# Gated linear attention and a maxout feed-forward on one core: the planner's load times, and when a small token group is opened

## The chip, the cores and the metric

The kernel runs on one core of a Trainium2 chip, in one launch. The metric is the device time of that launch in microseconds (us). The time before is 162.61 us, the median of three runs (162.48 to 163.09).

## The reference, cut to what matters

```python
# q, k, v, alpha: (4, 8, 768, 48) float32; w1, w2: (384, 1024); w_out: (1024, 384)
for t in range(S):
    state = alpha[:, :, t, :, None] * state + einsum('bhd,bhe->bhde', k[:, :, t], v[:, :, t])
    y[:, :, t] = einsum('bhd,bhde->bhe', q[:, :, t], state)
x = y.transpose(0, 2, 1, 3).reshape(3072, 384)
out = maximum(x @ w1, x @ w2) @ w_out
```

The first half is a recurrence over time with one state of 48 x 48 for each batch and head. The second half is a feed-forward over 3072 tokens.

## The kernel before, in words

**Chunks.** The recurrence is cut into 24 chunks of 128 time steps (six for each of four batches), all eight heads together. A chunk needs four loads of 192 KB (alpha, k, q, v: tiles `af`, `kf`, `qf`, `vf`), each with six buffers, issued from SP's queue at L184. The steps of chunk n, with the names that this text uses:

- a1(n), ACT, L252: the logarithm of alpha, `loga`. It is the first reader of the loads.
- p1(n), PE, L257 and L261: running sums of `loga`, `cs`. Then ACT makes two exponentials of it, `en` and `ep` (L267), and a small one, `gg` (L271).
- `kt` (POOL, L279) and `qt` (DVE, L276) scale k and q; POOL also casts v (L283).
- p2(n), PE, L316 and L318: transposes into `tp`; ACT or DVE copies them to `qk` (L393).
- p3(n), PE, L334: scores `pa`, `pb`; DVE masks them into `pt` (L353).
- kv(n), PE, L345: the chunk's addition to the state; DVE adds it (`w`, L364), POOL decays the state for the next chunk (L295, L303).
- p4(n), PE, L376 and L382: the output `y`; a3(n), ACT, L389, copies it into `xT`, the input of the feed-forward.

**Token groups.** The feed-forward uses max(a, b) = (a - b, floored at 0) + b: the weights w1 - w2 are made once (`wd`), and `m` = w2 @ w_out once. It runs over groups of one to three chunks. A group has eight steps f (PE, L429: three matmuls each into `h`, as wide as the group; then a relu on ACT, L436, or DVE, L434, into `g`), and for each chunk two steps t (PE): the first half has six matmuls (L443 and three of L446), the second five (L446), into `op`. `op` is evicted to `outs` (L393) and stored from SP's queue (L456). In this text f(i) and t(i) are numbered over the whole kernel, from 0 to 95 and from 0 to 23.

**What sets the order.** A small planner runs in Python when the kernel is built. It keeps a clock for each engine, gives every step a cost and a latency, and picks for each engine the step that can start first by its own sums; the earliest over all engines is emitted. Each engine then executes its instructions in that order, and waits where an input is not there. For SP the planner models a load as `LOAD` on a shared wire plus a latency `lat`. PE prefers steps of the recurrence; steps f and t have a high `prio` number and fill in. The function `refill` opens a token group when fewer than three steps of the last one are pending: it takes up to three chunks whose a3 is done, and as few as one.

Of the kernel before, what the change touches and what calls it, by code (L numbers as in the profile page):

```python
# [49 lines left out]
class Sched:  # L50
# [49 lines left out]
    def run(self):  # L100
        while True:
            c = self.pick("PE")
            if c and self.refill:
                self.refill(c[1])
            best = None
            for e in self.todo:
                c = self.pick(e)
                if c and (best is None or c[1] < best[0]):
                    best = (c[1], e, c[2])
            if best is None:  # L110
                if self.refill and self.refill(1e9):
                    continue
                break
            t, e, op = best
            cost = op.engs[e]
            if e == "PE" and op.tiled != self.tiled:
                cost += 0.09
                self.tiled = op.tiled
            if e == "SP":
                t = max(t, self.wire - 4.0)  # L120
                self.wire = max(self.wire, t + 0.7) + cost
                op.done = self.wire + op.lat
                cost = 0.45
            else:
                op.done = t + cost + op.lat
            self.free[e] = t + cost
            for b in op.alloc:
                b.ring.taken.append(b)
            for x in op.engs:
                self.todo[x].remove(op)  # L130
            op.fn(e)
        assert not any(self.todo.values()), {e: [(o.name, o.n) for o in v][:5] for e, v in self.todo.items()}
# [3 lines left out]
def kernel(  # L136
# [20 lines left out]
    C = 128  # L157
# [6 lines left out]
    WMAX = 384  # L164
# [15 lines left out]
    def load(n, i):  # L180
        b, c = divmod(n, NCH)
        src, tag = SRC[i]
        t = loads[n][i] = ldp.tile([128, H, D], FP32, tag=tag, name=tag)
        nc.sync.dma_start(out=t, in_=src[b, :, c * C : (c + 1) * C, :].rearrange("h p d -> p h d"))  # L184
# [58 lines left out]
    st = {n: {} for n in range(NCG)}  # L243
# [156 lines left out]
    def prep_t(f):  # L400
        tp = psx.tile([128, 2 * NP, 128], FP16, tag="x", name="wtp")
        for i in range(2):
            for s in range(3):
                nc.tensor.transpose(tp[:, 3 * i + s, :], w216[:, s, (f + i) * 128 : (f + i + 1) * 128], ident16)
        st["w2", f] = tp
# [18 lines left out]
    def fstep(a, W, f):  # L424
        if f == 0:
            gts[a] = mo.tile([128, NF, WMAX], FP16, tag="g16", name="g16", bufs=NG)
        h = hs[a, f] = psm.tile([128, WMAX], FP32, tag="m", name="h")
        for s in range(3):
            nc.tensor.matmul(h[:, 0:W], lhsT=wd16[:, s, f * 128 : (f + 1) * 128], rhs=xT[:, s, a : a + W],  # L429
                             start=(s == 0), stop=(s == 2))  # L430

    def relu(e, a, W, f):
        if e == "DVE":
            nc.vector.tensor_relu(gts[a][:, f, 0:W], hs[a, f][:, 0:W])  # L434
        else:
            nc.scalar.activation(out=gts[a][:, f, 0:W], in_=hs[a, f][:, 0:W], func=ACTF.Relu)  # L436

    def tstep(a, i, half):
        t0 = a + i * C
        if half == 0:  # L440
            op = ops[t0] = psm.tile([128, DM], FP32, tag="m", name="op")
            for s in range(3):
                nc.tensor.matmul(op, lhsT=xT[:, s, t0 : t0 + C], rhs=m16[:, s, :], start=(s == 0), stop=False)  # L443
        op = ops[t0]
        for f in (range(3) if half == 0 else range(3, NF)):
            nc.tensor.matmul(op, lhsT=gts[a][:, f, i * C : (i + 1) * C], rhs=wo16[:, f, :],  # L446
                             start=False, stop=(f == NF - 1))
# [3 lines left out]
    def oevict(e, t0):  # L451
        outs[t0] = mo.tile([128, DM], FP32, tag="outs", name="outs", bufs=NO)
        copy(e, outs[t0], ops[t0])

    def store(t0):
        nc.sync.dma_start(out=out[t0 : t0 + C, :], in_=outs[t0])  # L456
# [11 lines left out]
    def op(*a, **k):  # L468
        return Op(S, *a, **k)

    G = {n: {} for n in range(NCG)}

    def dep(n, name):
        return G[n].get(name) if n in G else None

    LOAD, WLOAD = 0.98, 3.9
    bl = {}

    def loads_of(n):
        bl[n] = [Buf(r) for r in rl]  # L480
        for i in range(4):
            G[n]["ld", i] = op("ld", n, {"SP": LOAD}, lambda e, n=n, i=i: load(n, i), lat=1.6, alloc=[bl[n][i]],
                               after=[G[n].get(("ld", i - 1)), dep(n - 1, ("ld", 3))], prio=n)

    loads_of(0)
    lw2 = op("w2", 0, {"SP": WLOAD}, lambda e: load_w2(), lat=1.6, after=[G[0]["ld", 3]], prio=0.5)
    prev = lw2
# [7 lines left out]
    for n in range(1, NCG):  # L495
        loads_of(n)
        if n == 1:
            G[1]["ld", 0].after.append(prev)
# [4 lines left out]
        for s, c in enumerate(({"ACT": 0.95}, {"DVE": 0.65}, {"POOL": 1.5}))  # L503
    ]
    wdc = [[op("wd", s, {"POOL": 1.2} if s == 2 else {"DVE": 0.68}, lambda e, s=s, i=i: prep_wd(e, s, i),
               deps=[lw1[i], lw2]) for s in range(3)] for i in range(2)]
# [4 lines left out]
    for f in range(0, NF, 2):  # L511
        b = Buf(rx)
        t = op("w2t", f, {"PE": 0.4}, lambda e, f=f: prep_t(f), lat=0.17, deps=w2c, alloc=[b], prio=500 + f)
# [3 lines left out]
    for s in range(3):  # L517
        b = Buf(rm)
        for i in range(2):
            prev = op("m", s, {"PE": 0.66}, lambda e, s=s, i=i: prep_m(s, i), lat=0.17,  # L520
                      deps=w2t + woc[2 * i : 2 * i + 2], after=[prev], alloc=[b] if i == 0 else (), prio=800 + s)
        mdone.append(op("mev", s, {"ACT": 0.4, "DVE": 0.45}, lambda e, s=s: copy(e, m16[:, s, :], mps[s]),
                        deps=[prev], reads=[b]))
# [4 lines left out]
    for n in range(NCG):  # L528
        c = n % NCH
# [28 lines left out]
        if c:  # L558
            pg = G[n - 1]
            add("g", {"POOL": 0.25}, lambda e, n=n: vg(n), [pg["gg"], g["gg"]], alloc=["g"], reads=[B_[n - 1]["gg"], "gg"])  # L560
            if c < NCH - 1:
                add("t32", {"POOL": 0.56}, lambda e, n=n: vt32(n), [g["g"], pg["w"]], alloc=["t32"],
                    reads=["g", B_[n - 1]["w"]])
            for t in range(2):
                add(f"T{t}", {"POOL": 0.56}, lambda e, n=n, t=t: vT(n, t), [g["g"], pg["w"]],
                    alloc=["T"] if t == 0 else (), reads=["g", B_[n - 1]["w"]] + (["T"] if t else []))
                if t:
                    g["T1"].after.append(g["T0"])
        if c < NCH - 1:
            add("kv", {"PE": 0.18}, lambda e, n=n: p3k(n), [g["kt"], g["v1"]], lat=0.17, alloc=["kv"], reads=["kt", "v"])  # L570
            add("w", {"DVE": 0.75}, lambda e, n=n: vw(n), [g["kv"], g.get("t32")], alloc=["w"],
                reads=["kv"] + (["t32"] if c else []))
        add("p4", {"PE": 0.54 if c else 0.37}, lambda e, n=n: p4(n), [g["m1"], g["v1"], g.get("T1")], lat=0.17,
            alloc=["y"], reads=["pt", "v", "qk"] + (["T"] if c else []), tiled=True)
# [3 lines left out]
    nxt = [0]  # L578
    pend = []

    def refill(now):
        while pend and pend[0].done is not None:
            pend.pop(0)
        if len([o for o in pend if o.done is None]) > 2 or nxt[0] >= NCG:
            return
        a = nxt[0]
        k = 0
        while k < WMAX // C and a + k < NCG and G[a + k]["a3"].done is not None and G[a + k]["a3"].done <= now + 0.3:
            k += 1
        if k == 0:  # L590
            return
        nxt[0] += k
        W, a0 = k * C, a * C
        bg = Buf(rg16)
        rel = []
        xs = [G[a + i]["a3"] for i in range(k)]
        for f in range(NF):
            bh = Buf(rm)
            o = op("f", a, {"PE": 3 * max(W / 2400 + 0.0025, 0.07)}, lambda e, a0=a0, W=W, f=f: fstep(a0, W, f),
                   lat=0.17, deps=xs + wdc[f // NFH], after=pend[-1:], alloc=[bh] + ([bg] if f == 0 else []), prio=1000 + a)  # L600
            pend.append(o)
            rel.append(op("relu", a, {"ACT": 0.08 + W / 1200, "DVE": 0.1 + W / 960},
                          lambda e, a0=a0, W=W, f=f: relu(e, a0, W, f), deps=[o], reads=[bh, bg], prio=n))
        for i in range(k):
            bo, bs = Buf(rm), Buf(ro)
            for half in range(2):
                o = op("t", a + i, {"PE": (0.98, 0.82)[half]}, lambda e, a0=a0, i=i, half=half: tstep(a0, i, half),
                       lat=0.17, deps=mdone + woc + (rel[:3] if half == 0 else rel), after=pend[-1:],
                       alloc=[bo] if half == 0 else (), reads=[bg] if half else [bg], prio=1000 + a)
                pend.append(o)  # L610
            ev = op("oev", a + i, {"ACT": 0.4, "DVE": 0.45}, lambda e, t=a0 + i * C: oevict(e, t), deps=[o],
                    alloc=[bs], reads=[bo], prio=n)
            op("st", a + i, {"SP": 0.5}, lambda e, t=a0 + i * C: store(t), lat=1.2, deps=[ev], reads=[bs], prio=-1)
        return True

    S.refill = refill
# [31 lines left out]
```

## Time and profile before

| | |
|---|---|
| median of the runs | 162.61 us |
| the profiled execution | 162.2 us |
| its span, first to last instruction | 160.3 us |
| PE busy | 138.6 us (86%) |
| ACT busy | 101.8 us (64%) |
| POOL busy | 87.6 us (55%) |
| DVE busy | 81.9 us (51%) |
| DMA queue of the loads and stores | 84.9% of 16 engines' span |
| mean granted TensorE clock | 0.968 |

Busy time counts instructions that run; an engine that stands in front of a semaphore is idle. The span is that of one execution; the 1.9 us around it belong to every run. PEld are the weight loads of TensorE, which run beside its matmuls. In rows of a timeline the first number is the start in us from the beginning of the span, the second how long it lasted; in brackets stands how long the engine was idle just before, and what ended that.

### The profile page before, as it was taken

What the parts mean: (1) busy time and instruction counts of PE and PEld (TensorE: products, weight loads), DVE (VectorE), ACT (ScalarE), POOL (GpSimd) and SP (SyncE); (2) the same over time, 40 slices, a digit from 0 to 9 for tenths busy, and PEclk for the clock granted to TensorE, in tenths of its full rate; (3) what the DMA queues carried; (4) which work ended last, traced back from release to release, by engine and by line L of the source; (5) the groups of instructions that cost most, each with busy time, mean ns of one, the idle gap of its engine ahead of it and who ended that gap; (6) DMA issues with size and microseconds to landing.
All of it is one profiled execution on the core that took longest, in us unless ns stands there. A gap on an engine that the chain in (4) does not pass through costs nothing.

```text
span 160.3 us, 5013 instructions
## 1 busy us (share of the span) xinstructions
PE 138.6 (86%) x2000; PEld 93.7 (58%) x2000; DVE 81.9 (51%) x162; ACT 101.8 (64%) x242; POOL 87.6 (55%) x170
## 2 busy tenths in 40 slices
PE   0355999599759999999899999798999999999991
PEld 0324755486535776776566667375666665666760
DVE  4466826376500989383575596554988721000100
ACT  3336674495726887778787678666785658374441
POOL 7708217778472679685697679337969910000000
PEclk9999999869955999999999999999999999999999
DMA  5999989998989999979999999799999411120302
GB/s 106 274 364 393 317 132 203 189 181 176 205 176 215 193 206 183 209 149 206 197 251 179 192 208 228 162 197 188 212 217 225 111 49 49 53 98 0 131 16 98
DMA packets 105318, 28.62 MB, mean 179 GB/s; under 512 B 100304, under 2 KB 104400, under 8 KB 105168
## 3 DMA queue, kind: packets, MB, share of 16 engines
q1 hardware_dynamic: 105296, 28.32, 84.9%
q8 instruction: 15, 0.25, 0.7%
q14 instruction: 7, 0.06, 0.1%
HBM read 23.59 MB, written 4.72 MB: 177 GB/s over the span
## 4 chain that ended last, share of the span: by engine, by line
PE 46%; SPq 22%; DMA 18%; ACT 5%; DVE 4%; issue 2%; POOL 1%; ACTq 0%
SPq L184 19%; DMA af<-in_alpha_dram 18%; PE h L429 13%; PE op L446 12%; PE op L443 5%; PE y L382 3%; PE pa L334 2%; PE y L376 2%; ACT loga L252 2%; PE tp L316 2%; DVE pt L353 2%; PE tp L318 2%; PE cs L257 2%; PE kv L345 1%; ACT g L436 1%
## 5 line engine op out<-in xcount | busy, mean ns | idle before, releaser
L429 PE MATMUL h<-xT,wd 128*128 128x128 f16 (+2 forms) x288 | 41.3, 284 | 1.6 <-DVE wd L398 0.8
L446 PE MATMUL op<-wo,g 128*128 128x384 f16 x192 | 38.5, 334 | 0.0
L279 POOL TENSOR_TENSOR kt<-kf,en 128x384 f16<-128x384 f32 x24 | 25.3, 1053 | 16.4 <-ACT en L267 15.7
L283 POOL CAST v<-vf 128x192 f16<-128x192 f32 x48 | 22.7, 478 | 16.9 <-DMA vf<-in_v_dram 10.3
L436 ACT ACTIVATE g<-h 128x384 f16<-128x384 f32 (+2 forms) x76 | 28.0, 397 | 4.8 <-PE h L429 4.2
L429 PEld LDWEIGHTS <-wd 128*128 128x128 f16 x288 | 24.2, 104 | 10.8 <-DVE wd L398 1.5
L446 PEld LDWEIGHTS <-g 128*128 128x128 f16 x192 | 18.2, 99 | 12.1 <-issue 0.8
L252 ACT ACTIVATE loga<-af 128x384 f16<-128x384 f32 x24 | 12.5, 522 | 19.6 <-DMA af<-in_alpha_dram 19.5
L393 ACT COPY qk<-tp 128x1024 f16<-128x1024 f16 x20 | 20.3, 1013 | 6.5 <-PE tp L318 6.4
L295 POOL TENSOR_TENSOR T<-w,g 48x192 f16<-48x192 f32 x40 | 20.5, 512 | 1.6
L353 DVE TENSOR_TENSOR pt<-pa,u 128x512 f16<-128x512 f32 x24 | 16.5, 690 | 8.3 <-PE pb L334 7.1
L443 PE MATMUL op<-m,xT 128*128 128x384 f16 x72 | 16.1, 334 | 2.2 <-ACT g L436 2.2
L434 DVE TENSOR_SCALAR g<-h 128x128 f16<-128x128 f32 (+2 forms) x20 | 7.3, 379 | 20.5 <-PE h L429 20.3
L276 DVE TENSOR_TENSOR qt<-qf,ep 128x384 f16<-128x384 f32 x24 | 16.1, 673 | 3.0 <-DMA qf<-in_q_dram 1.7
L364 DVE TENSOR_TENSOR w<-kv,t 48x192 f32<-48x192 f32 x32 | 11.3, 353 | 12.2 <-PE kv L345 9.6
L382 PE MATMUL y<-pt,v 128*32 128x128 f16 x576 | 16.0, 230 | 1.1 <-DVE pt L353 1.1
L353 DVE TENSOR_TENSOR pt<-pb,u 128x512 f16<-128x512 f32 x24 | 16.4, 681 | 0.1
L393 ACT COPY outs<-op 128x384 f32<-128x384 f32 x17 | 8.1, 474 | 11.9 <-PE op L446 11.9
L257 PE MATMUL cs<-loga,cmat 128*128 128x384 f16 x24 | 8.1, 339 | 8.4 <-ACT loga L252 8.4
L389 ACT CAST xT<-y 128x384 f16<-128x384 f32 x24 | 11.6, 483 | 5.0 <-PE y L382 5.0
L382 PEld LDWEIGHTS <-v 128*32 128x32 f16 x576 | 12.1, 102 | 2.2 <-issue 2.1
L267 ACT ACTIVATE en<-cs 128x384 f32<-128x384 f32 x24 | 12.0, 499 | 2.0 <-PE cs L261 1.7
(58 smaller groups left out, 189.7 us busy)
## 6 DMA issues: line engine op xcount, KB each, us to landing
af<-in_alpha_dram SPq DMA_DIRECT2D x24, 192.0 KB, 4.4
kf<-in_k_dram SPq DMA_DIRECT2D x24, 192.0 KB, 4.3
qf<-in_q_dram SPq DMA_DIRECT2D x24, 192.0 KB, 4.5
vf<-in_v_dram SPq DMA_DIRECT2D x24, 192.0 KB, 4.4
out_dram<-outs SPq DMA_DIRECT2D x24, 192.0 KB, 3.0
w2f<-in_moe_w_dram SPq DMA_DIRECT2D x1, 1536.0 KB, 7.9
w1f<-in_moe_w_dram SPq DMA_DIRECT2D x2, 768.0 KB, 9.7
wof<-in_moe_w_out_dram SPq DMA_DIRECT2D x2, 768.0 KB, 12.3
```

What stands on the lines that cost most here:

```text
L184: nc.sync.dma_start(out=t, in_=src[b, :, c * C : (c + 1) * C, :].rearrange("h p d -> p h d"))
L276: nc.vector.tensor_mul(out=qts[n % 2][:, :, 0:D], in0=loads[n][2], in1=st[n]["ep"])
L279: nc.gpsimd.tensor_mul(out=kts[n % NB][:, :, 0:D], in0=loads[n][1], in1=st[n]["en"])
L283: nc.gpsimd.tensor_copy(out=v16s[n % NB][:, :, :, 32 * t : 32 * t + 16], in_=vp[:, t])
L295: nc.gpsimd.tensor_mul(out=st[n]["T16"][ps, :, :, 16 * t : 16 * t + 16], in0=st[n - 1]["w"][ps].rearrange("p (r s) e -> p r s e", s=3), in ...
L353: nc.vector.tensor_mul(out=s["pt"][:, t], in0=s["pp"][t], in1=ub)
L382: nc.tensor.matmul(y[32 * r : 32 * r + 32, i, :], lhsT=v16[:, r, i, 16 * t : 16 * t + 32], rhs=s["pt"][:, t, r, :], start=(first and t == ...
L393: {"ACT": nc.scalar.copy, "DVE": nc.vector.tensor_copy, "POOL": nc.gpsimd.tensor_copy}[e](out=out, in_=in_)
L429: nc.tensor.matmul(h[:, 0:W], lhsT=wd16[:, s, f * 128 : (f + 1) * 128], rhs=xT[:, s, a : a + W], start=(s == 0), stop=(s == 2))
L436: nc.scalar.activation(out=gts[a][:, f, 0:W], in_=hs[a, f][:, 0:W], func=ACTF.Relu)
L443: nc.tensor.matmul(op, lhsT=xT[:, s, t0 : t0 + C], rhs=m16[:, s, :], start=(s == 0), stop=False)
L446: nc.tensor.matmul(op, lhsT=gts[a][:, f, i * C : (i + 1) * C], rhs=wo16[:, f, :], start=False, stop=(f == NF - 1))
```

## The change

Four edits, all in what the planner believes and when a group is opened; no step is computed in another way.

1. The wire cost of a load goes from 0.98 to 1.06, that of a store from 0.5 to 0.55.
2. The latency of a load, 1.6 for all, grows with the chunk: 1.6 for chunks 0 and 1, 2.1 for chunk 2, 2.6 for chunk 3, 3.1 from chunk 4 on.
3. `refill` opens a group of one or two chunks only if PE, by the planner's clock, would otherwise stand for more than 0.3.
4. When nothing else can be planned, `refill` is told that PE is idle.

```diff
@@ run
             c = self.pick("PE")
             if c and self.refill:
-                self.refill(c[1])
+                self.refill(c[1], c[1] > self.free["PE"] + 0.3)
...
             if best is None:
-                if self.refill and self.refill(1e9):
+                if self.refill and self.refill(1e9, True):
                     continue
@@ the kernel's function
-    LOAD, WLOAD = 0.98, 3.9
+    LOAD, WLOAD = 1.06, 3.9
...
-            G[n]["ld", i] = op("ld", n, {"SP": LOAD}, lambda e, n=n, i=i: load(n, i), lat=1.6, alloc=[bl[n][i]],
+            G[n]["ld", i] = op("ld", n, {"SP": LOAD}, lambda e, n=n, i=i: load(n, i), lat=1.6 + min(1.5, max(0.0, 0.5 * (n - 1))), alloc=[bl[n][i]],
...
-    def refill(now):
+    def refill(now, idle):
...
-        if k == 0:
+        if k == 0 or (k < WMAX // C and not idle):
             return
...
-            op("st", a + i, {"SP": 0.5}, lambda e, t=a0 + i * C: store(t), lat=1.2, deps=[ev], reads=[bs], prio=-1)
+            op("st", a + i, {"SP": 0.55}, lambda e, t=a0 + i * C: store(t), lat=1.2, deps=[ev], reads=[bs], prio=-1)
```

The order is the same up to the last of the `m` matmuls and p2(1); from there on every engine's order differs. Three places follow.

ACT around a1(6), the logarithm of chunk 6 (written to `loga_106`). Before:

```order
L267 ACTIVATE en<-cs 128x384
L436 ACTIVATE g_713<-h 128x128
L267 ACTIVATE ep<-cs 128x384
L436 ACTIVATE g_713<-h 128x128
L271 ACTIVATE gg<-cs 128x8
L252 ACTIVATE loga_106<-af 128x8x48
L436 ACTIVATE g_713<-h 128x128 x3
L393 COPY qk<-tp 128x1024
L389 CAST xT<-y 128x3x128
L267 ACTIVATE en<-cs 128x384
```

Now:

```order
L267 ACTIVATE en<-cs 128x384
L389 CAST xT<-y 128x3x128
L267 ACTIVATE ep<-cs 128x384
L271 ACTIVATE gg<-cs 128x8
L252 ACTIVATE loga_106<-af 128x8x48
L436 ACTIVATE g_867<-h 128x128 x4
L267 ACTIVATE en<-cs 128x384
L436 ACTIVATE g_867<-h 128x128
L267 ACTIVATE ep<-cs 128x384
L271 ACTIVATE gg<-cs 128x8
```

Before, the last three relus of the third group stand behind this a1; now that group's relus are all ahead of it, and the first four of the fourth group, f(24) to f(27), stand behind it.

PE at p1(23), the last chunk's running sums. Before (row 3364 of PE's 4002, 638 behind it):

```order
L345 LDWEIGHTS kt_111
L345 MATMUL kv<-v_1_114,kt_111 128x96
L257 LDWEIGHTS cmat
L257 MATMUL cs<-loga_107,cmat 128x384
L261 LDWEIGHTS loga_107
L261 MATMUL cs<-gcol,loga_107 128x2
```

Now (row 3460, 542 behind it):

```order
L318 LDWEIGHTS kt_111
L318 MATMUL tp<-ident_87,kt_111 128x128
L257 LDWEIGHTS cmat
L257 MATMUL cs<-loga_107,cmat 128x384
L261 LDWEIGHTS loga_107
L261 MATMUL cs<-gcol,loga_107 128x2
```

It stands 96 rows (48 matmuls) later: before, it came behind f(71), both halves of t(13), and kv(19); now behind f(79), the first half of t(16) and p2(22), with kv(19) after it.

SP around the load of alpha for chunk 23, the last `af` of each piece. Before:

```order
L184 DMA kf<-in_k_dram 128x8x48
L456 DMA out_dram<-outs 128x384
L184 DMA qf<-in_q_dram 128x8x48
L184 DMA vf<-in_v_dram 128x8x48
L184 DMA af<-in_alpha_dram 128x8x48
L456 DMA out_dram<-outs 128x384
L184 DMA kf<-in_k_dram 128x8x48
L184 DMA qf<-in_q_dram 128x8x48
L184 DMA vf<-in_v_dram 128x8x48
L456 DMA out_dram<-outs 128x384
L184 DMA af<-in_alpha_dram 128x8x48
L184 DMA kf<-in_k_dram 128x8x48
```

Now:

```order
L184 DMA af<-in_alpha_dram 128x8x48
L456 DMA out_dram<-outs 128x384
L184 DMA kf<-in_k_dram 128x8x48
L184 DMA qf<-in_q_dram 128x8x48
L184 DMA vf<-in_v_dram 128x8x48
L456 DMA out_dram<-outs 128x384
L184 DMA af<-in_alpha_dram 128x8x48
L184 DMA kf<-in_k_dram 128x8x48
L456 DMA out_dram<-outs 128x384
```

Counted over SP's whole queue, 13 stores stood ahead of this load; now 15 do, and one more between it and the last load.

## The prediction

> **What bounds the kernel now.** I read the page first, then the waits, then the work of the engines by stage, then single rows of the timelines and the end of the chain.
>
> ```profile
> span 160.3 us, 5013 instructions
> PE 138.6 (86%) x2000; PEld 93.7 (58%) x2000; DVE 81.9 (51%) x162; ACT 101.8 (64%) x242; POOL 87.6 (55%) x170
> ...
> DMA  5999989998989999979999999799999411120302
> ...
> SPq L184 19%; DMA af<-in_alpha_dram 18%; PE h L429 13%; PE op L446 12%; PE op L443 5%; PE y L382 3%; PE pa L334 2%; PE y L376 2%; ACT loga L252 2%; PE tp L316 2%; DVE pt L353 2%; PE tp L318 2%; PE cs L257 2%; PE kv L345 1%; ACT g L436 1%
> ```
>
> PE is the fullest engine, but 37% of the chain is SP's queue and the alpha loads. DMA is full until about 124 us (31 slices of 4 us), then nearly idle, while PE goes on alone to the end. So there are two stages: one in which loads set the pace, and one of PE work left over.
>
> ```profile
> 24.75:52.40 27.65, 22.76 (x352) 16.09 (x353) 12.59 (x27) 16.42 (x43) 18.16 (x36) 0.81 1.16 192
> 52.40:124.60 72.20, 69.19 (x1207) 47.35 (x1204) 50.47 (x98) 55.13 (x137) 53.43 (x100) 1.00 1.04 200
> 124.60:156.90 32.30, 32.23 (x323) 20.19 (x320) 5.25 (x10) 17.72 (x39) 4.09 (x9) 1.00 0.20 67
> ```
>
> The columns are the stage, its length, then busy time of PE, PEld, DVE, ACT and POOL, the granted clock, DMA's share, GB/s. From 24.75 to 124.60 PE idles 4.89 + 3.01 = 7.90 us; afterwards never. 124.60 is the start of p1(23), the last step that reads a load of alpha.
>
> ```profile
> ACT loga L252 <- DMA af<-in_alpha_dram: 19.5, 17, 1.9
> ...
> PE cs L257 <- ACT loga L252: 8.4, 7, 4.4
> ...
> PE op L443 <- ACT g L436: 2.2, 1, 2.2
> ```
>
> The waits: ACT stands 19.5 us, 17 times of 24, in front of an alpha that has not landed, with everything else in its queue behind. PE inherits part of it, in two forms:
>
> ```profile
> 77.83 0.32 PE L257 MATMUL cs<-loga,cmat 128*128 128x384 f16 x1 [0.57 <-ACT loga L252]
> ...
> 101.92 0.32 PE L257 MATMUL cs<-loga,cmat 128*128 128x384 f16 x1 [0.94 <-ACT loga L252]
> ...
> 110.56 0.32 PE L257 MATMUL cs<-loga,cmat 128*128 128x384 f16 x1 [0.67 <-ACT loga L252]
> ...
> 45.75 1.12 PE L443 MATMUL op<-m,xT 128*128 128x384 f16 x3 [2.25 <-ACT g L436]
> ```
> ```profile
> 45.01 0.52 ACT L252 ACTIVATE loga<-af 128x384 f16<-128x384 f32 x1 [1.82 <-DMA af<-in_alpha_dram]
> 45.44 0.59 ACT L436 ACTIVATE g<-h 128x128 f16<-128x128 f32 x3
> ```
>
> The first three are p1(13), p1(18) and p1(20), direct. In the last t(2) waits for relus that are done in 0.59, but stand behind a1(6), which waited for its load. Such waits cost twice, for the granted clock (column before DMA's share) falls:
>
> ```profile
> 28.00:32.00 4.00, 1.97 (x50) 1.58 (x49) 1.57 (x3) 1.90 (x3) 2.95 (x7) 0.89 1.39 189
> 32.00:36.00 4.00, 4.00 (x74) 3.47 (x74) 2.88 (x7) 3.54 (x11) 2.86 (x6) 0.69 1.39 184
> ...
> 44.00:48.00 4.00, 2.25 (x10) 1.24 (x10) 0.49 (x1) 1.02 (x4) 2.94 (x7) 0.59 0.85 175
> 48.00:52.00 4.00, 4.00 (x61) 2.37 (x58) 0.16 (x1) 2.77 (x5) 1.15 (x2) 0.55 1.17 218
> ```
>
> Lost clock: 4 x (0.11 + 0.31) = 1.7 us in the first pair, 4 x (0.41 + 0.45) = 3.4 in the second. At half clock 1.64 of the stretch 44:48 means that it began near 44.7, so about 0.5 of the 3.4 was lost while PE stood anyway; 2.9 count.
>
> **The change, part by part.** Instructions are the same in kind and number: 288 matmuls of h in 12 token groups before and after. The widths change: groups of 1, 2, 3 chunks were 5, 2, 5, now 4, 4, 4. Two pairs replace one single and one triple. So the third part does not make groups wider on the whole. What that costs:
>
> ```profile
> 38.88 0.50 PE L429 MATMUL h<-xT,wd 128*128 128x128 f16 x6
> 39.22 0.39 PE L316 MATMUL tp<-ident,qt 128*128 128x128 f16 x4
> ```
> ```profile
> 124.60 0.17 PE kv L345 x4
> ...
> 135.16 0.49 PE op L443 x3
> 135.65 0.49 PE op L446 x3
> ...
> 136.77 0.92 PE op L446 x5
> 137.68 0.49 PE op L443 x3
> 138.17 1.30 PE op L446 x8
> ...
> 141.26 3.90 PE h L429 x24
> ...
> 150.52 2.74 PE h L429 x24
> ...
> 156.91 0.48 ACT outs L393
> ```
>
> A step f of one chunk takes 0.17 (39.22 - 38.88 for two), of two chunks 2.74 / 8 = 0.34, of three 3.90 / 8 = 0.49. One single and one triple: 8 x 0.66 = 5.3; two pairs: 5.5. A loss of 0.2, and the count of relus is the same 96, so I set it at nothing; its cover is that the other terms are rounded to more.
>
> The whole effect is where the steps stand. From PE's order, behind p1(23) stood 16 steps f of three chunks, 8 of two, and t(14) to t(23); now 8 of three, 8 of two, the second half of t(16), t(17) to t(23), and one kv. So 8 steps f (8 x 0.49 = 3.92), three first halves of t (0.49 + 0.49 = 0.98 each, 2.94) and two second halves (1.30 - 0.49 = 0.81 each, 1.62) went ahead of it, and one kv (0.17) behind: 8.3 us less PE work behind p1(23). What is left behind it runs without a wait, as 32.23 of 32.30 did, so:
>
> end = start of p1(23) + (32.3 - 8.3) + 3.4 (the last eviction and store, 160.3 - 156.9).
>
> The start of p1(23) has two bounds.
>
> *Loads.*
>
> ```profile
> 118.83 0.91 SPq L456 DMA_DIRECT2D out_dram<-outs  x1
> 119.80 0.42 SPq L184 DMA_DIRECT2D af<-in_alpha_dram  x1
> ```
> ```profile
> 123.60 0.52 ACT L252 ACTIVATE loga<-af 128x384 f16<-128x384 f32 x1 [1.15 <-DMA af<-in_alpha_dram]
> ```
> ```profile
> L456 SPq DMA_DIRECT2D out_dram<-outs x24: 332/580/2594, 33.8 to 157.4; - x24
> ```
>
> af(23) was issued at 119.80 and waited for until 123.60; with the 0.52 of a1 and a handover, p1(23) could not start before 124.2. SP's queue is moved too: 15 stores stand ahead of af(23) where 13 stood. Nothing shows that DMA has room for them there. A store holds SP for 0.58 at the median (0.33 to 2.59, which bound it); two at the median give 1.2: 125.4. The lower end is 124.2, since issue rows behind a store are short (0.42); the upper end is two at the longest, 129.4.
>
> *PE.* It must do 8.3 more by then: 124.6 + 8.3 = 132.9, less the losses that go. Idle time up to 52.4 was 4.89. By the moment when the relus behind a1(6) run (45.4), PE's order now has f(24) to f(26) and all of t(2) done besides what it had: 3 x 0.17 + 1.79 = 2.3. So 2.6 remain. Nothing goes at 28 to 31, where it idled twice:
>
> ```profile
> 26.35 0.33 PE L257 MATMUL cs<-loga,cmat 128*128 128x384 f16 x1
> ...
> 29.03 0.40 PE L316 MATMUL tp<-ident,qt 128*128 128x128 f16 x4 [1.02 <-DVE qt L276]
> ...
> 30.66 0.32 PE L257 MATMUL cs<-loga,cmat 128*128 128x384 f16 x1 [1.01 <-ACT loga L252]
> ...
> 40.23 0.32 PE L257 MATMUL cs<-loga,cmat 128*128 128x384 f16 x1 [0.40 <-ACT loga L252]
> ```
>
> p1(2) now stands behind t(0)'s second half and p3(1), some 1.1 later, and p2(2) needs what comes 2.7 after it; p4(1), put between, covers only part. I keep 2.0 of idle and the 1.7 of slow clock that follow. The other 0.6 is what is left of 2.25 + 0.40 + small ones near 45, at a1(6), which still stands ahead of four relus. With so little idle there, the second fall of the clock (2.9) goes. PE's waits for a1 after 52.4 are 8.4 - 4.4 (the first chunk) - 1.01 - 0.40 = 2.6, four of the seven. Between p1(7) and p1(13), the first of the four, the order puts 14.6 us of f and t now, 13.2 before; between p1(7) and p1(20), the last, 34.9 now, 29.0 before: 1.4 more at the first, where 0.57 was waited, and 5.9 at the last, against 2.6 in all. So PE comes to p1 after the load, not ahead of it. I keep 1.1 of the 3.01: the 0.4 that no a1 caused and one wait of the mean size (0.65), since a1 on ACT is what is late next. Idle falls from 7.9 to 3.7, by 4.2. So 132.9 - 4.2 - 2.9 = 125.8.
>
> ACT gives eight of its 76 relus to DVE (3.2 us at its 0.40 each), and DVE, busy 81.9 of 160.3, has room: set at nothing. If that cover is gone, masks (DVE's pt) come later and with them p4.
>
> ```profile
> L436 ACT ACTIVATE g<-h 128x384 f16<-128x384 f32 (+2 forms) x76 | 28.0, 397 | 4.8 <-PE h L429 4.2
> ```
>
> PE's bound, 125.8, is the later. The span: 125.8 + 24.0 + 3.4 = 153.2. The profiled execution took 162.2 with a span of 160.3, so 1.9 lie around it: 155.1. The median of the runs, 162.61, is 0.4 above that execution: **155.5 us**.
>
> **A rule against a row.** Gaps of 1.02 and 1.01 within 28:32, and one of 2.25 near 45, each went ahead of a half clock. The Trainium skill, TensorE: Matmul & The Clock Gate, section "Why this matters for your kernels", asks that PE not idle for more than about 3 us between bursts, one idle window being what throttles. The trace disagrees: no gap after 25 us is longer than 2.25. By that rule the clock would not fall in the changed kernel at all; by the rows a gap of one or two microseconds can do it, and I go by the rows.
>
> **Rivals.**
> *The second fall of the clock stays* (PE stands 1.5 or more near a1(6), which is still ahead of four relus): 2.9 more, 158.4. For: four relus stand behind that load, and PE has no other filler then. Against: 2.3 us of work were put ahead.
> *The clock stays full.* The 1.7 at 31 to 35 goes too, PE's bound falls to 124.1, and the loads' 125.4 decides: 0.4 less, 155.1. That is what the Trainium skill's page TensorE: Matmul & The Clock Gate would make of gaps this short. Against: the 28:32 row, whose idle time I see no cover for.
> *It does not do what it says:* planned idle goes, but ACT still stands 19.5 us for alpha and hands it to PE through relus and qk copies; each gap filled opens another. Then nothing of 4.2 + 2.9 is won, p1(23) starts at 132.9 and the end is as before, 162.6. For: the alpha that ACT waits for is paced by DMA, which the change does not quicken. Against: PE now has work in front.
> *Slower:* stores and loads share SP's queue in order. A store waits for its eviction, that for PE; if PE lags the planner, the 15 stores ahead of af(23) hold loads back. At 0.7 each it is 10.5: p1(23) at 134.7, the end at 164.4. It decides from 0.6 each on (15 x 0.6 = 9.0 against 132.9 - 124.2 = 8.7). For: the longest store held SP 2.59. Against: the median, 0.58, includes the issue itself.
>
> **How the numbers follow.** Forecast (153.5 to 157.5) 0.52; clock falls again (to 160.5) 0.22; clock full, 155.1, 0.08; nothing won, 0.08; slower 0.06; loads land earlier than in this trace and it ends under 153.5, 0.04. The range, 153.5 to 160.5, holds the first three, 0.82: its low end is p1(23) at 124.2 (24.0 + 3.4 + 2.3 behind it make 153.9) and a little for the rounding; its high end the second fall of the clock and two more microseconds of the loads' upper end. Under 0.5% (0.8 us) a measurement of this kernel tells nothing from no change; so faster 0.86, same 0.08, slower 0.06.
>
> **What would show it.** PE work behind p1(23) about 24 us; p1(23) starting at 125 to 127; ACT's wait for alpha well under 19.5 us; PE's wait for a1 after 52 us under 1; half clock only once after 25 us; af(23) issued near 121. Wrong if p1(23) starts after 130, through a second fall of the clock, or with SP held by stores.

## The result, and the profile after

The changed kernel takes 155.44 us (median of four runs, 154.26 to 155.5), beside 162.55 for the kernel before on the same chip (162.07 to 163.09). The ratio is 0.9544, with a 95% interval of 0.949 to 0.9599: faster by 4.6%. The profiled execution took 155.42 us with a span of 153.6, so 1.8 lie around it. 155.5 was forecast.

From the page of the changed kernel, the busy times, the granted clock and DMA in 40 slices, and the chain by engine and by line:

```profile
span 153.6 us, 5006 instructions
PE 136.4 (89%) x2000; PEld 92.9 (61%) x2000; DVE 89.4 (58%) x170; ACT 99.7 (65%) x234; POOL 88.6 (58%) x170
...
PEclk9999999969999999999999999999999999999999
DMA  5999999998989898989899999799989993111302
...
PE 56%; DMA 18%; DVE 6%; ACT 5%; SPq 5%; issue 4%; POOL 3%; ACTq 0%; DVEq 0%; POOLq 0%
PE op L446 15%; PE h L429 15%; DMA af<-in_alpha_dram 12%; PE op L443 6%; DMA w1f<-in_moe_w_dram 6%; SPq L184 4%; PE y L382 3%; PE pa L334 3%; PE tp L316 3%; PE tp L318 2%; DVE qt L276 2%; PE y L376 2%; PE cs L257 2%; PE kv L345 2%; DVE wd L398 2%
```

SP's queue and the alpha loads, 37% of the chain before, are 16% now. DMA is full until about 126 us (33 slices of 3.84), 2 us longer than before, and the mostly idle stretch behind that is shorter. In time, the work of the engines by stage, cut at p2(1), near 52, and at p1(23):

```profile
24.49:52.00 27.51, 25.66 (x445) 18.66 (x446) 17.70 (x34) 18.94 (x53) 18.86 (x37) 0.94 1.14 196
52.00:126.22 74.22, 72.68 (x1160) 49.12 (x1159) 52.51 (x100) 54.34 (x128) 53.99 (x101) 1.00 1.01 200
126.22:150.10 23.88, 23.87 (x274) 15.21 (x271) 5.30 (x10) 13.85 (x30) 3.73 (x7) 1.00 0.21 66
```

p1(23) starts 1.6 us later than before, at 126.22, and 23.88 us of PE work stand behind it where 32.30 stood. So the kernel does not run through its loads sooner; it does more of the feed-forward while it waits for them. Before p1(23) PE idles 1.85 + 1.54 = 3.39 us, where it was 7.90. The waits (us in total, times, the longest):

```profile
ACT loga L252 <- DMA af<-in_alpha_dram: 11.4, 12, 2.1
...
PE cs L257 <- ACT loga L252: 5.6, 5, 4.4
```

ACT's wait for alpha fell from 19.5 to 11.4 us, PE's wait for a1, without the first chunk's 4.4, from 4.0 to 1.2.

### The profile page after: what moved, and what is told of

Its sections match the earlier page's. It is cut to its first block, busy times and chain, and to the rows that moved or that the text cites. A ratio compares the mean times of both kernels' runs of the same rounds, so it can differ in the third digit from the quotient of the medians.

```text
span 153.6 us, 5006 instructions
## 1 busy us (share of the span) xinstructions
PE 136.4 (89%) x2000; PEld 92.9 (61%) x2000; DVE 89.4 (58%) x170; ACT 99.7 (65%) x234; POOL 88.6 (58%) x170
## 3 DMA queue, kind: packets, MB, share of 16 engines
q1 hardware_dynamic: 105296, 28.32, 87.7%
## 4 chain that ended last, share of the span: by engine, by line
PE 56%; DMA 18%; DVE 6%; ACT 5%; SPq 5%; issue 4%; POOL 3%; ACTq 0%; DVEq 0%; POOLq 0%
PE op L446 15%; PE h L429 15%; DMA af<-in_alpha_dram 12%; PE op L443 6%; DMA w1f<-in_moe_w_dram 6%; SPq L184 4%; PE y L382 3%; PE pa L334 3%; PE tp L316 3%; PE tp L318 2%; DVE qt L276 2%; PE y L376 2%; PE cs L257 2%; PE kv L345 2%; DVE wd L398 2%
## 5 line engine op out<-in xcount | busy, mean ns | idle before, releaser
L279 POOL TENSOR_TENSOR kt<-kf,en 128x384 f16<-128x384 f32 x24 | 24.0, 999 | 24.7 <-ACT en L267 13.4
L446 PE MATMUL op<-wo,g 128*128 128x384 f16 x192 | 37.5, 326 | 0.0
L283 POOL CAST v<-vf 128x192 f16<-128x192 f32 x48 | 24.1, 510 | 10.9 <-DMA vf<-in_v_dram 7.6
L436 ACT ACTIVATE g<-h 128x128 f16<-128x128 f32 (+2 forms) x68 | 24.4, 383 | 5.3 <-PE h L429 4.6
L446 PEld LDWEIGHTS <-g 128*128 128x128 f16 x192 | 17.7, 98 | 11.5
L276 DVE TENSOR_TENSOR qt<-qf,ep 128x384 f16<-128x384 f32 x24 | 19.4, 809 | 4.6 <-ACT ep L267 2.4
L295 POOL TENSOR_TENSOR T<-w,g 48x192 f16<-48x192 f32 x40 | 21.1, 528 | 1.5
L364 DVE TENSOR_TENSOR w<-kv,t 48x192 f32<-48x192 f32 x32 | 11.4, 355 | 16.6 <-PE kv L345 12.9
L252 ACT ACTIVATE loga<-af 128x384 f16<-128x384 f32 x24 | 12.7, 528 | 11.5 <-DMA af<-in_alpha_dram 11.4
L434 DVE TENSOR_SCALAR g<-h 128x256 f16<-128x256 f32 (+2 forms) x28 | 11.6, 427 | 13.3 <-PE h L429 13.2
L382 PE MATMUL y<-pt,v 128*32 128x128 f16 x576 | 15.4, 222 | 1.7 <-DVE pt L353 1.7
```

Source lines behind the costliest of these rows:

```text
L252: nc.scalar.activation(out=logas[n % 2][:, :, 0:D], in_=loads[n][0], func=ACTF.Ln)
L276: nc.vector.tensor_mul(out=qts[n % 2][:, :, 0:D], in0=loads[n][2], in1=st[n]["ep"])
L279: nc.gpsimd.tensor_mul(out=kts[n % NB][:, :, 0:D], in0=loads[n][1], in1=st[n]["en"])
L283: nc.gpsimd.tensor_copy(out=v16s[n % NB][:, :, :, 32 * t : 32 * t + 16], in_=vp[:, t])
L295: nc.gpsimd.tensor_mul(out=st[n]["T16"][ps, :, :, 16 * t : 16 * t + 16], in0=st[n - 1]["w"][ps].rearrange("p (r s) e -> p r s e", s=3), in ...
L382: nc.tensor.matmul(y[32 * r : 32 * r + 32, i, :], lhsT=v16[:, r, i, 16 * t : 16 * t + 32], rhs=s["pt"][:, t, r, :], start=(first and t == ...
```

## The experiments

The question behind them: which of the four edits moves the work, and why does it pay? The main theory is that loads set when p1(23) can run, that the end is this moment plus the PE work behind it, and that the assumed load cost decides how much that is. The rivals: the gain comes from ACT (relus and copies no longer stand behind an a1 that waits) and from the clock; or from the group rule or the latency. The load cost and the store cost of edit 1 were only moved together, so their shares stay open.

For each kernel, from its profile: the start of p1(23), PE's work behind it, and PE's idle time from p2(1) to p1(23).

| kernel | median us | ratio to before (95%) | p1(23) | PE behind it | PE idle ahead of it |
|---|---|---|---|---|---|
| before | 162.55 | | 124.60 | 32.2 | 7.9 |
| after | 155.44 | 0.9544 (0.949 to 0.9599) | 126.22 | 23.9 | 3.4 |
| cost | 157.12 | 0.9558 (0.9481 to 0.9636) | 127.71 | 23.9 | 5.4 |
| lat | 164.12 | 0.9989 (0.9939 to 1.004) | 125.92 | 33.6 | 12.6 |
| refill | 161.13 | 0.9812 (0.9732 to 0.9891) | 125.27 | 30.8 | 10.4 |
| cost_refill | 157.42 | none | 125.24 | 24.3 | 4.4 |
| a1late | 164.13 | 1.0037 (1.0005 to 1.007) | 127.80 | 32.2 | 12.2 |
| quick_before | 151.55 | 0.9276 (0.924 to 0.9312) | 113.64 | 32.2 | 2.2 |
| quick_after | 151.71 | 0.9296 (0.9254 to 0.9339) | 122.23 | 23.9 | 2.2 |
| again (as after) | 155.32 | 0.9542 (0.9468 to 0.9615) | 126.64 | 23.9 | 4.2 |
| load110 | 154.39 | 0.9528 (0.9461 to 0.9596) | 125.61 | 22.0 | 1.7 |
| load114 | 155.71 | 0.9613 (0.9563 to 0.9663) | 130.70 | 18.9 | 3.1 |
| load118 | 157.28 | 0.9703 (0.9647 to 0.976) | 135.86 | 15.5 | 3.2 |
| wide | 154.97 | 0.9506 (0.9468 to 0.9545) | 130.45 | 18.3 | 3.0 |

The idle time is the length of the stage from p2(1) to p1(23) less PE's busy time in it. Ratios are taken against the kernel before on the same chip, whose median was 162.55 to 164.2; medians of different chips are not compared. Six times came out above the ranges that the main theory gave them, by 0.1 to 1.1 us (cost, lat, cost_refill, a1late and both kernels with quick loads), and so did the span of wide, by 0.3; on the chip of cost, lat, refill and cost_refill the kernel before itself took 164.2. cost, by 0.1, and cost_refill, by 0.9, thereby fall between the theory and its rivals. The misses that count are those of load114 and load118, below.

### Edit 1 alone: the costs

```diff
-    LOAD, WLOAD = 0.98, 3.9
+    LOAD, WLOAD = 1.06, 3.9
...
-            op("st", a + i, {"SP": 0.5}, lambda e, t=a0 + i * C: store(t), lat=1.2, deps=[ev], reads=[bs], prio=-1)
+            op("st", a + i, {"SP": 0.55}, lambda e, t=a0 + i * C: store(t), lat=1.2, deps=[ev], reads=[bs], prio=-1)
```

> One part alone: the planner's wire cost of a load (1.06) and of a store (0.55); latency and the rule for small groups as before. Theory W (the end is the start of p1(23) plus the PE work that stands behind it): counted from the order, 23.5 us stand behind p1(23), as in the changed kernel (23.4; before 31.7). With p1(23) at 125.5 to 127 the time is 155 to 157. Rival G (the gain comes from not opening small groups): under half the gain, 159 or more. Rival L (it comes from the later latency, which takes ACT's wait for alpha away): 159 or more.

The work by stage of this kernel, up to p1(23) and behind it:

```profile
25.27:127.71 102.44, 97.04 (x1651) 66.83 (x1652) 70.34 (x130) 71.41 (x187) 72.15 (x138) 1.00 1.01 195
127.71:151.70 23.99, 23.90 (x227) 14.29 (x224) 4.33 (x8) 13.53 (x30) 3.26 (x6) 1.00 0.22 70
```

The ratio, 0.9558, is the whole change's within the intervals. The work behind p1(23) is as short as the changed kernel's, and ACT still waits about as long for alpha as before:

```profile
ACT loga L252 <- DMA af<-in_alpha_dram: 19.1, 17, 2.6
```

So the gain doesn't need ACT to wait less. Nor does it need the clock: the four runs of this kernel, at a granted clock of 0.999 to 1.000, took 155.63 to 157.41 us; six runs of the kernel before on the same chip, at 0.998 to 1.000, took 162.58 to 164.47.

### Edit 2 alone: the latency

```diff
-            G[n]["ld", i] = op("ld", n, {"SP": LOAD}, lambda e, n=n, i=i: load(n, i), lat=1.6, alloc=[bl[n][i]],
+            G[n]["ld", i] = op("ld", n, {"SP": LOAD}, lambda e, n=n, i=i: load(n, i), lat=1.6 + min(1.5, max(0.0, 0.5 * (n - 1))), alloc=[bl[n][i]],
```

> One part alone: the planner's latency of a load grows to 3.1; costs and groups as before. Theory W: 32.4 us of PE work stand behind p1(23), 0.7 more than before, and p1(23) cannot start before its load allows it, about 124.2: 162.5 to 164. Rival L: most of the gain, 159 or less.

The same view:

```profile
24.28:125.92 101.64, 89.03 (x1558) 61.21 (x1559) 67.03 (x132) 70.00 (x176) 71.13 (x138) 1.00 1.03 192
125.92:160.00 34.08, 33.63 (x340) 20.71 (x339) 5.20 (x10) 18.49 (x44) 3.32 (x7) 1.00 0.22 71
```

Nothing: a ratio of 0.9989, and the interval holds 1. This profiled execution took 1.1 us more than the median, so its stages are read for the split and not to the tenth. A latency that is added once to a load leaves the pace of the loads that the planner believes in as it was; it puts no more PE work ahead of p1(23).

### Edits 3 and 4 alone: the group rule

```diff
-                self.refill(c[1])
+                self.refill(c[1], c[1] > self.free["PE"] + 0.3)
...
-                if self.refill and self.refill(1e9):
+                if self.refill and self.refill(1e9, True):
...
-    def refill(now):
+    def refill(now, idle):
...
-        if k == 0:
+        if k == 0 or (k < WMAX // C and not idle):
```

> One part alone: a group of one or two chunks is opened only if PE would stand by the planner's clock; costs and latency as before. Six groups of three chunks come out, two of two, two of one. Theory W: 30.3 us stand behind p1(23), 1.3 less than before: 160 to 162. Rival G: most of the gain, 158 or less.

The same view:

```profile
24.68:125.27 100.59, 90.23 (x1521) 61.16 (x1522) 65.12 (x121) 69.45 (x169) 69.38 (x135) 1.00 1.01 193
125.27:156.10 30.83, 30.82 (x309) 18.55 (x306) 5.47 (x10) 17.98 (x38) 4.67 (x9) 1.00 0.24 73
```

The ratio is 0.9812 (0.9732 to 0.9891): faster, though whether by 2% is unclear. 1.4 us less stand behind p1(23), which is the same road, but not the whole 1.9%, or 3.1 us. This kernel also has 10 groups, so 240 matmuls of h and not 288; what that is worth was not measured apart. Together with the costs the rule brings nothing that can be seen:

### Edits 1, 3 and 4: all but the latency

> Two parts: the costs and the rule for groups, without the later latency. Theory W: 23.8 us behind p1(23), 0.4 more than in the changed kernel: 155 to 156.5. Rival L: without the latency the waits for alpha return: 158 or more.

The four runs took 154.86 to 157.43, median 157.42, too few and too far apart for a ratio. Its profiled execution, the quickest of them, has 24.32 of PE work behind a p1(23) at 125.24. The median lies between what the theory allowed (up to 156.5) and what the rival asked (158 or more), so it decides neither, and the latency's part in the whole change is under what these runs tell.

### The kernel before, with each a1 only just ahead of its p1

```diff
-            op.fn(e)
+            self.made.append((op, e))
...
+    for n in range(1, NCG):
+        x = next(m for m in S.made if m[0] is G[n]["a1"])
+        S.made.remove(x)
+        S.made.insert(next(i for i, m in enumerate(S.made) if m[0] is G[n]["p1"]), x)
+    for o, e in S.made:
+        o.fn(e)
```

PE's order is that of before; on ACT each a1 now stands behind the relus and copies that stood behind it.

> The kernel before, with every a1(n) moved in the emitted order to just ahead of p1(n), so that on ACT it stands behind the relus, copies and evictions that were planned between the two; PE's order of steps is the same as before. Theory W: 31.7 us still stand behind p1(23), which its load holds to about 124.2: 161.8 to 163. Rival A (PE lost time because ACT's queue stood behind an early a1, 2.25 us at t(2), and the clock fell for it, 2.9): 157 to 159.

Its waits, then its work by stage:

```profile
PE cs L257 <- ACT loga L252: 13.9, 18, 4.5
ACT loga L252 <- DMA af<-in_alpha_dram: 4.9, 6, 2.0
```
```profile
25.31:127.80 102.49, 90.33 (x1555) 61.44 (x1556) 66.87 (x126) 73.62 (x180) 71.75 (x138) 1.00 0.99 192
127.80:160.10 32.30, 32.23 (x319) 20.17 (x318) 4.40 (x9) 17.29 (x38) 3.23 (x6) 1.00 0.19 65
```

The rival that lays the gain to ACT falls. ACT's 19.5 us in front of alpha went down to 4.9, and PE took part of them over (8.4 to 13.9 in front of a1). The clock didn't fall at all (1.00), and the ratio is 1.0037 (1.0005 to 1.007). A queue that no longer waits, and a full clock, win nothing while the load is late and the same work stands behind it.

### Both orders with quick loads

```diff
-        nc.sync.dma_start(out=t, in_=src[b, :, c * C : (c + 1) * C, :].rearrange("h p d -> p h d"))
+        flat = src.rearrange("b h s d -> (b h s d)").rearrange("(n p f) -> n p f", p=128, f=H * D)
+        nc.sync.dma_start(out=t.rearrange("p h d -> p (h d)"), in_=flat[n])
```

The same bytes come as 128 runs of 1536 bytes and not 1024 of 192, in another arrangement. So these two kernels compute other values than the reference, and serve only to time the two orders. Lines behind this one shift by one.

> The kernel before, in the same order, but each load takes 128 runs of 1536 bytes instead of 1024 of 192, the same bytes in number from the same tensors, in another arrangement, so that it computes with other values in the chunks. A store of that shape took 0.58 us of DMA time, a load 1.12. Theory W: loads then come earlier than the planner thinks, p1 never waits, and PE alone sets the end: 24.8 us of start, somewhat less, 114.5 of work, 5 of small losses, 3.4 at the end, 2.2 around: 147 to 151. Rival O (the order of before is worse in itself, through ACT and the buffers of h): more than 3 us above the changed kernel's order with the same loads.

> The changed kernel with the same quick loads (other values in the chunks). Theory W: within 1.5 us of the order of before with quick loads, 147 to 151: an order is good or bad only against the loads. Rival O: it keeps 3 us or more of its lead.

The work by stage, first with the order before, then with the changed one:

```profile
24.12:113.64 89.52, 87.30 (x1555) 60.90 (x1556) 63.53 (x124) 71.32 (x180) 73.87 (x138) 1.00 0.67 209
113.64:145.90 32.26, 32.23 (x323) 20.18 (x320) 5.20 (x10) 17.52 (x39) 3.23 (x6) 1.00 0.17 60
```
```profile
23.93:122.23 98.30, 96.13 (x1603) 66.32 (x1604) 70.22 (x133) 72.47 (x180) 73.28 (x137) 1.00 0.63 196
122.23:146.20 23.97, 23.87 (x274) 15.20 (x271) 5.30 (x10) 13.86 (x31) 3.73 (x7) 1.00 0.17 58
```

This settles what the order is worth. With loads out of the way the order before has p1(23) 11 us earlier than with slow ones, its 32.23 behind it cost nothing, and both orders take the same time (0.9276 and 0.9296, intervals overlapping). PE idles 2.2 us in both. The 4.6% are not in the order as such but in how it fits the pace of the loads.

### The changed kernel again, and costs further up

`again` is the changed kernel unchanged; load110, load114 and load118 differ from it in one number, 1.1, 1.14 or 1.18.

```diff
-    LOAD, WLOAD = 1.06, 3.9
+    LOAD, WLOAD = 1.1, 3.9
```

> The changed kernel again, on the same chip as the next three: 154 to 157, depending on the chip (on one where the kernel before takes 164, two of its parts took 157).

> The changed kernel with the planner's cost of a load at 1.10 instead of 1.06. Counted from the order, 21.5 us of PE work stand behind p1(23), 1.9 less than at 1.06. Theory W: the load's bound (about 125.5) still holds p1(23), and the end comes 0.5 to 1.8 earlier than the changed kernel on the same chip. Rival P (a planner that thinks loads later than they are pays for it, with loads lying in their buffers and PE at the end short of work): the same or slower.

> The same with 1.14. 17.6 us behind p1(23). Theory W: the load no longer holds p1(23), which comes at 128.5 to 130, PE's idle time goes to the 2.3 us that quick loads left, and the end is 1 to 3 us earlier than the changed kernel's, no more, since PE's own work is then the bound (149.4 of span with quick loads). Rival P: later than at 1.10.

> The same with 1.18. 14.4 us behind p1(23). Theory W: as at 1.14 within 1 us, p1(23) at 131 to 133: work moved ahead of a step that PE reaches late anyway changes nothing. Rival P: 1.5 us or more slower than at 1.14.

Work by stage at 1.10, and the stage up to p1(23) at 1.18:

```profile
24.40:125.61 101.21, 99.56 (x1617) 70.03 (x1618) 66.95 (x129) 75.48 (x186) 71.75 (x134) 0.98 1.07 203
125.61:147.70 22.09, 22.00 (x259) 13.50 (x256) 6.43 (x11) 12.61 (x28) 5.19 (x11) 1.00 0.16 56
```
```profile
25.79:135.86 110.07, 106.89 (x1786) 77.06 (x1786) 71.07 (x143) 80.81 (x211) 73.82 (x138) 1.00 0.97 191
```

At 1.10 PE idles 1.7 us ahead of p1(23), and only 22 stand behind it. The median is the lowest of these four, yet its interval (0.9461 to 0.9596) overlaps those of the changed kernel and of its repetition, so no gain is shown. From 1.14 on p1(23) is no longer where the loads put it but later, at 130.7 and 135.9, because PE has that much other work planned ahead of it. What stands behind falls by less (18.9 and 15.5), and the ratio rises to 0.9613 and 0.9703. The theory had 1.14 at 1 to 3 us ahead of `again` and 1.18 within 1 us of 1.14. Instead 1.14 took 0.4 us more than `again`, with overlapping intervals (0.9563 to 0.9663 beside 0.9468 to 0.9615), and 1.18 another 1.6, its interval (0.9647 to 0.976) clear of those of `again` and 1.10. So a slower assumed pace does not go on costing nothing: 1.18 shows that, and 1.14 shows at least that nothing more is won.

### Late p1(23) with few groups

1.14 and 1.18 bring two things: p1(23) is late, and the planner opens more groups, 15 and 16 instead of 12. This kernel is late with 12.

```diff
-    LOAD, WLOAD = 1.06, 3.9
+    LOAD, WLOAD = 1.1, 3.9
...
-            G[n]["ld", i] = op("ld", n, {"SP": LOAD}, lambda e, n=n, i=i: load(n, i), lat=1.6 + min(1.5, max(0.0, 0.5 * (n - 1))), alloc=[bl[n][i]],
+            G[n]["ld", i] = op("ld", n, {"SP": LOAD}, lambda e, n=n, i=i: load(n, i), lat=1.6, alloc=[bl[n][i]],
...
-            op("st", a + i, {"SP": 0.55}, lambda e, t=a0 + i * C: store(t), lat=1.2, deps=[ev], reads=[bs], prio=-1)
+            op("st", a + i, {"SP": 0.7}, lambda e, t=a0 + i * C: store(t), lat=1.2, deps=[ev], reads=[bs], prio=-1)
```

> The planner's load at 1.10, store at 0.70, latency as before. As much PE work stands ahead of p1(23) as with a load cost of 1.14 (17.7 us behind it; there 17.6), but in 12 token groups of widths 1 to 3 instead of 15 of 1 and 2. Theory S (what made 1.14 and 1.18 slower than 1.10 is the greater number of small groups: 360 and 384 matmuls of h instead of 288): a span of 150 to 152, as at 1.10, and a ratio of 0.94 to 0.955 to the kernel before. Rival P (it is the lateness of p1 itself): as at 1.14, a span of 153 or more, a ratio of 0.96 or more.

Its work up to p1(23), and the costliest group, the matmuls of h, of this kernel, of 1.14 and of 1.18 (behind the count busy us in all and mean ns, then PE's idle time before them):

```profile
25.25:130.45 105.20, 102.23 (x1665) 69.87 (x1666) 68.79 (x133) 78.24 (x185) 74.07 (x138) 1.00 0.99 195
```
```profile
L429 PE MATMUL h<-xT,wd 128*128 128x128 f16 (+2 forms) x288 | 39.3, 280 | 1.7 <-DVE wd L398 0.8 <-ACT xT L389 0.4 <-ACT g L436 0.3
```
```profile
L429 PE MATMUL h<-xT,wd 128*128 128x256 f16 (+1 forms) x360 | 41.4, 257 | 2.7 <-ACT g L436 1.0 <-DVE wd L398 1.0 <-ACT outs L393 0.5
```
```profile
L429 PE MATMUL h<-xT,wd 128*128 128x256 f16 (+1 forms) x384 | 41.8, 251 | 3.4 <-ACT g L436 1.4 <-DVE wd L398 0.8 <-ACT xT L389 0.6
```

p1(23) is as late as at 1.14, at 130.45, with as much idle time ahead of it (3.0 and 3.1), and yet the ratio is 0.9506, its interval wholly under 1.14's. So a late p1(23) costs little by itself, and what is left points at the small groups. The same columns take 360 matmuls and 41.4 us where 288 took 39.3. Of PE's busy time the two kernels differ by 1.2 us in all (120.55 beside 121.79, p2(1) to the end); rows overlap, so the groups don't add up to it exactly. The kernel differs from 1.14 in the latency and the store cost too, so what is shown is that a late start with few groups does not cost what 1.14 does; that the group count alone is the cause is not shown. Its interval (0.9468 to 0.9545) overlaps that of the changed kernel (0.949 to 0.9599): no version here is shown to beat it.

## Why the prediction was right

**The work behind p1(23)** was forecast at 24.0 and measured 23.88; it runs without a wait, as said. The tail of 3.4 is 153.59 - 150.10 = 3.5.

**The start of p1(23)**, forecast 125.8 by PE's bound, is 126.22. Its rows on ACT and PE in the changed kernel:

```profile
125.02 0.52 ACT L252 ACTIVATE loga<-af 128x384 f16<-128x384 f32 x1
...
126.22 0.33 PE L257 MATMUL cs<-loga,cmat 128*128 128x384 f16 x1
```

Neither waits, so alpha was there and PE's bound was the later, as chosen: a1(23) ends at 125.54, 0.7 before PE comes to p1(23). Its terms can be read from the two stages ahead of it. Busy time there grew from 22.76 + 69.19 = 91.95 to 25.66 + 72.68 = 98.34, by 6.4; idle time fell by 4.5; the stage starts 0.3 earlier: 124.60 + 6.4 - 4.5 - 0.3 = 126.2. The forecast had 8.3 - 2.9 = 5.4 of busy time and 4.2 of idle time.

- *The idle time*, 4.2 forecast, 4.5 measured, but not in the places named. After 52 us, 1.54 stayed (1.1 was kept); at 28:32, 1.1 (2.0 was kept); near 45 nearly nothing (0.6 was kept); and 0.46 between 36 and 40, where none was named. The eight relus that went to DVE, set at nothing, are a likely part: up to 52 us PE waits 0.6 for DVE's masks (pt) and 0.5 for a relu on DVE, and in the kernel before, from 24.7 on, for neither. The sign that PE's waits for a1 after 52 us would be under 1 was missed: they are 1.2. The windows around both falls of the clock before:

```profile
28.00:32.00 4.00, 2.89 (x54) 2.41 (x54) 2.54 (x4) 2.45 (x8) 3.47 (x7) 0.77 1.43 187
32.00:36.00 4.00, 3.97 (x43) 2.75 (x41) 2.59 (x5) 2.59 (x10) 3.35 (x7) 0.80 1.06 193
44.00:48.00 4.00, 3.88 (x90) 2.97 (x85) 3.97 (x7) 3.36 (x15) 3.85 (x8) 1.00 0.89 168
48.00:52.00 4.00, 4.00 (x75) 2.76 (x74) 2.74 (x6) 2.00 (x5) 1.04 (x3) 1.00 1.07 201
```

- *The clock*: in the profiled execution the second fall is gone and the first is there, 4 x (0.23 + 0.20) = 1.7 us, both as said. That the first is there is partly luck: the other three runs of the changed kernel had a granted clock of 0.998 to 1.000 and took 154.26 to 155.5 us. The profiled execution of `again`, the same order, ran at 1.00 and has 97.06 + 23.86 = 120.9 us of PE busy, 1.3 less than the 122.2 here, but more idle time, and p1(23) at 126.64. The size of the second fall, 2.9, is not confirmed. From p2(1) on the kernel before has 91.95 + 32.23 = 124.2 us of PE busy, and with quick loads, at full clock, 87.30 + 32.23 = 119.5: the difference, 4.7, is near 1.7 + 2.9. But a1late, at full clock with slow loads, has 90.33 + 32.23 = 122.6, so 3.0 of such a difference can come without any fall of the clock.

```profile
25.46:126.64 101.18, 97.06 (x1603) 66.43 (x1604) 71.06 (x133) 73.19 (x180) 72.55 (x137) 1.00 1.03 198
```

- *The busy time*, work less clock, is the term that was too small, by 1.0. Half of it is the order itself: with quick loads the changed one takes 96.13 + 23.87 = 120.0 us of PE, 0.5 more than the one before. The two pairs in place of a single and a triple, worked out at 0.2 and set at nothing, are part of this; what else is was not isolated. The other half shows only with slow loads: 98.34 + 23.87 = 122.2 is 2.2 over 120.0, and the clock makes 1.3 (by `again`) to 1.7 (by the granted clock) of that. Whether the rest is work or a second fall priced too high stays open.

**a1(6) and the relus behind it.** The feared wait didn't come. ACT's rows there in the changed kernel:

```profile
44.05 0.56 ACT L252 ACTIVATE loga<-af 128x384 f16<-128x384 f32 x1
44.53 0.97 ACT L436 ACTIVATE g<-h 128x128 f16<-128x128 f32 x4
```

**SP's queue.** af(23) was forecast to be issued near 121.0 and was issued at 121.61:

```profile
119.83 1.72 SPq L456 DMA_DIRECT2D out_dram<-outs  x1
121.61 0.43 SPq L184 DMA_DIRECT2D af<-in_alpha_dram  x1
```
```profile
L456 SPq DMA_DIRECT2D out_dram<-outs x24: 332/761/2271, 31.0 to 150.7; - x24
```

That is 1.8 later than before, where the two more stores were put at 1.2: the median store now holds SP for 0.76 us where it was 0.58 (shortest, median and longest in ns in the last row). The rival by which stores hold back the loads was said to decide from 0.6 each on. 0.76 is above that, and it didn't decide. Its point was set wrong: it counted all 15 stores as new, and 13 had been there before.

**Where the sum was lucky.** The span, 153.6, came out 0.4 above the 153.2 of the sum, and the 0.4 added for the median over the profiled execution was not there (155.44 beside 155.42). Within p1(23), 1.0 too little busy time is offset by 0.3 more idle time gone and by a stage that starts 0.3 earlier, which nothing forecast. The mechanism held; that the time is right to 0.1 is chance.

**What the prediction didn't see** is how little the clock matters by itself. In a1late, lat and refill the clock didn't fall (1.00 up to p1(23)), PE idled 10 to 13 us, and p1(23) started within 3.2 us of where it was. While the loads set the pace, a full clock only turns slow rows into idle time. That a fall less could be won here, because more work stood ahead of p1(23), is an argument that no run tests. The prediction's loads' bound, 125.4, was what limited such gains, and it lay so near PE's 125.8 that the time would have come out right whichever held. "Nothing won", at 0.08, needed PE to stand for each us that was filled; PE stood 3.4.

## What to carry to other kernels

Where loads set the pace up to a last step that reads one, the end is that step plus what is left behind it, so count the work behind it first; filling waits ahead of it pays only through that count. A planner that believes in loads 8% quicker than it needs to (0.98 beside 1.06) cost 4.4% here (edit 1 alone, in which the store cost moved too). The trace had the price: 1.12 us of DMA time for a load and 0.58 for a store (the figures in what was expected of quick_before), where the planner had 0.98 and 0.5 and now has 1.06 and 0.55. Believing in slower loads made no difference that can be told up to 1.14 and cost again at 1.18, where the planner also cut the filler into more and smaller pieces.

## What the runs showed of the hardware that was not expected

**Short runs of bytes set the pace.** The queue of the loads (packets, MB, share of 16 engines' span) with the order before and quick loads:

```profile
q1 hardware_dynamic: 19280, 28.32, 58.3%
```

The same 28.32 MB took 84.9% of 160.3 us before, 136 us of 16 engines, and 58.3% of 149.4 here, 87 us. SP issued the quicker loads in a shorter time too, 0.42 us at the median beside 0.76 for the loads of alpha (shortest, median and longest in ns; first the quick loads, then the kernel before):

```profile
L185 SPq DMA_DIRECT2D af<-in_alpha_dram x24: 327/425/4772, 0.7 to 104.1; - x24
```
```profile
L184 SPq DMA_DIRECT2D af<-in_alpha_dram x24: 425/755/4702, 0.7 to 119.8; - x24
```

The instruction is the same and only the runs of bytes differ, and no view lists what makes the row longer.

**The clock differs between runs of one program, without a clear difference in time.** On the chip of the four partial kernels the one before ran at a granted clock of 0.998 to 1.000 in six runs (162.58 to 164.47 us) and of 0.979 to 0.990 in six others (162.85 to 164.99). In the changed kernel's profiled execution it fell soon after 30 us, after these idle times of PE:

```profile
28.17 0.24 PE L382 MATMUL y<-pt,v 128*32 128x128 f16 x4 [0.26 <-DVE pt L353]
...
28.77 0.24 PE L382 MATMUL y<-pt,v 128*32 128x128 f16 x4 [0.36 <-DVE pt L353]
...
29.93 0.43 PE L316 MATMUL tp<-ident,qt 128*128 128x128 f16 x4 [0.58 <-DVE qt L276]
```

From 24.4 us to the fall none is longer than 0.58. The Trainium skill, TensorE: Matmul & The Clock Gate, section "Why this matters for your kernels", asks for no idle gaps of PE over about 3 us between bursts of matmuls; the prediction went by rows in which shorter gaps stood ahead of a fall, and these are shorter still. But the rows don't give the rule either: the profiled execution of `again`, of the same order, has the same three waits, 0.26, 0.36 and 0.58, and its clock stayed at 1.00; it was 1.000 in four of its six runs (153.66 to 155.84 us). So these gaps alone don't decide it. What makes the clock fall was not found.
